# The last phase of a three-stage kernel on pairs of 512 tokens instead of 384

## The chip, the cores and the metric

The kernel runs on one core of one Trainium2 chip. The metric is the device time of one execution, in microseconds (us); the time of a version is the median of several runs. TensorE (PE) multiplies matrices, VectorE (DVE) and ScalarE (ACT) work elementwise and read TensorE's results out of PSUM, GpSimd (POOL) works elementwise on SBUF alone, and SyncE (SP) issues nearly all DMAs.

## The reference

Three stages follow each other. 4 x 768 = 3072 tokens of width 512 go through all of them.

```python
x = attention(q, k, v, mem_k, mem_v)              # chunks of 32 tokens, 16 left, 8 right, 8 memory slots
h = x @ w_in                                      # 512 -> 2048
x = (max(h, 0) + log1p(exp(-abs(h)))) @ w_out     # 2048 -> 512
out = ((x @ w_a) * (x @ w_b)) @ w_out2            # 512 -> 1536, product, 1536 -> 512
```

## The kernel before, in words

All matrix products keep float32 accuracy by splitting each operand into a high and a low part (`hi`, `lo`) and adding three products: hi x hi, hi x lo and lo x hi. So one product of a 128-row slice takes three matmuls.

The first two stages run on eight tiles of `TT` = 384 tokens. In each tile, 16 slices `f` of the hidden width are computed one after the other: `emit_h` (L538, `ph`), `emit_soft` (ACT and DVE, with the split of the result into `gh` and `gl`), and two slices later `emit_x1` (L562, `px`). Attention for the tile after is laid between them. Each tile's result goes to DRAM (`x1d`, L571).

The last phase takes the tokens in four pairs of 384 (`p` = 0..3). The product of the pair with a 2 x 2 block arrangement of `w_a` and `w_b` is done with seven block products instead of eight (a Strassen-Winograd scheme): sums of token blocks (`add_pair`, L585) and of weight blocks (`Conversion`) are formed first, and `product` (L720) does one block product as 2 x 3 = 6 matmuls. For each of the 12 slices `f` of the width 1536, `pair_step` (L767) runs, in this order on TensorE: the block products "11" (bank `x`), "s2" (`y`), "s3" (`w`), "s1" (`v`), "12" (onto `x`), "22" (onto `w`), "s4" (onto `v`). DVE combines the banks into the sums `q`, `r`, `d22`, `d21`, `d12`, forms the two products `c2` and `c1` (the gated activations of the second and the first half of the pair), and splits them, with ACT, into `c`.

The last matmul of the model is cut into jobs (`job`, L739, `py`): a job takes 128 tokens of one half and two slices `f`, and is 2 x 3 = 6 matmuls of 512 columns; DVE adds its result to `y` (L758). Every second step adds six jobs to a list, and `next_job` takes three of them per step, one each after "s2", "s1" and "22". What is left when the steps end is done in a tail. 4 pairs x 6 groups x 6 jobs make 144 jobs; the very last is cut into two of 256 columns.

In the last phase the order on every engine is the order of the code (a manual schedule). `at(k)` (L955) is called after each block product and lays other work between: for pair 0 the conversion of the weights (POOL and ACT), later the loads of the converted weights (`fetch_u`, L712) and, in the steps `f` = 6 to 11 of a pair, the loads, sums and splits of the next pair's token blocks (`load_pair`, `add_pair`, `split_hi` on ACT, `split_lo` on DVE and POOL). For pair 0 these sums and splits stand in the last tile of the second stage (`plan2`, L898), all on DVE. The last two `emit_x1` run inside step 0 of pair 0.

Of the kernel before, what the change touches and what calls it, by code (L numbers as in the profile page):

```python
# [9 lines left out]
F32 = mybir.dt.float32  # L10
# [7 lines left out]
TT = 384  # L18

# [23 lines left out]
OUT_TAGS = "eegg"  # L43
# [3 lines left out]
GROUP = 2  # L47
# [3 lines left out]
def attn_moe_moe2(ctx: ExitStack, tc: tile.TileContext, q, k, v, mem_k, mem_v,  # L51
# [17 lines left out]
    NTILE = NT // TT  # L69
    KT = DM // P  # L70
# [8 lines left out]
    x1d = nc.dram_tensor("x1_scratch", (NTILE, P, KT, TT), F32, kind="Internal").ap()  # L79
# [463 lines left out]
    def emit_soft(t, f, ph, engine=nc.gpsimd, one=None, two=None):  # L543
        e = mp.tile([P, TT], F32, tag="e", name=f"e{t}_{f}")
        nc.scalar.activation(e, ph, AF.Abs)  # L545
        nc.scalar.activation(e, e, AF.Exp, scale=-1.0)  # L546
        nc.scalar.activation(e, e, AF.Ln, bias=1.0)  # L547
        g = mp.tile([P, TT], F32, tag="g", name=f"g{t}_{f}")
        nc.vector.scalar_tensor_tensor(g, ph, 0.0, e, ALU.max, ALU.add)  # L549
        if one:  # L550
            one()
        gt[t, f] = split(g, f"g{t}_{f}", engine, two)

    def emit_x1(t, f):
        gh, gl = gt.pop((t, f))
        w = w1o[f]
        if f == 0:
            acc[t] = [ps.tile([P, 512], F32, tag=f"acc{i}", name=f"px{t}_{i}", bufs=1) for i in range(KT)]
        for i in range(KT):
            wh, wl = w[:, 0, i * P:(i + 1) * P], w[:, 1, i * P:(i + 1) * P]  # L560
            for m, (a, c) in enumerate(((wh, gh), (wh, gl), (wl, gh))):
                nc.tensor.matmul(acc[t][i][:, :TT], lhsT=a, rhs=c, start=f == 0 and m == 0,  # L562
                                 stop=f == NF1 - 1 and m == 2)
        if f == NF1 - 1:
            for i in range(KT):
                if t == NTILE - 1:
                    o = wp.tile([P, TT], F32, tag="w", name=f"xo{t}_{i}")
                else:
                    o = mp.tile([P, TT], F32, tag=OUT_TAGS[i], name=f"xo{t}_{i}")
                nc.vector.tensor_copy(o, acc[t][i][:, :TT])  # L570
                nc.sync.dma_start(x1d[t, :, i, :], o)  # L571
            del acc[t]
# [7 lines left out]
    def load_pair(p):  # L580
        for n, (t, k) in {"11": (0, 0), "12": (0, 1), "21": (1, 0), "22": (1, 1)}.items():
            raws[n] = wp.tile([P, KH, TT], F32, tag="w", name=f"x{n}_{p}")
            nc.sync.dma_start(raws[n], x1d[2 * p + t, :, KH * k:KH * k + KH, :])

    def add_pair(engine, n):  # L585
        r = raws
        if n == "s1":
            r[n] = wp.tile([P, KH, TT], F32, tag="w", name="xs1")
            engine.tensor_tensor(r[n], r["21"], r["22"], ALU.add)
        elif n == "s2":  # L590
            r[n] = wp.tile([P, KH, TT], F32, tag="w", name="xs2")
            engine.tensor_tensor(r[n], r["s1"], r["11"], ALU.subtract)
        elif n == "s3":
            r[n] = r.pop("21")
            engine.tensor_tensor(r[n], r["11"], r[n], ALU.subtract)
        else:
            r["s4"] = wp.tile([P, KH, TT], F32, tag="w", name="xs4")
            engine.tensor_tensor(r["s4"], r["12"], r["s2"], ALU.subtract)

    def split_hi(p, n, copy):  # L600
        if n in ("22", "s4"):
            if (p, "2") not in parts:
                parts[p, "2"] = mp.tile([P, 2, 2, KH, TT], F32R, tag="x", name=f"xx{p}")
            sums[p, n] = parts[p, "2"][:, n == "s4"]
        else:
            sums[p, n] = late["x"].tile([P, 2, KH, TT], F32R, tag="s", name=f"x{n}_{p}")
        copy(sums[p, n][:, 0], raws[n])
# [125 lines left out]
    def temp(tag, name):  # L733
        return mp.tile([P, TT], F32, tag=tag, name=name, bufs=3 if tag in ("gh", "gl") else 2)
# [4 lines left out]
    def job(p, m, half, i, cols=slice(0, DM)):  # L739
# [27 lines left out]
    def pair_step(p, f, at, between=()):  # L767

        late_lo = pair_step.late
        x = bank("h", f"pX{p}_{f}")  # L770
        product(x, p, f, "11", True)
        s = temp("e", f"s{p}_{f}")
        nc.scalar.copy(s, x[:, :TT])
# [3 lines left out]
        q = temp("gh", f"q{p}_{f}")  # L777
        tt(q, y[:, :TT], s, ALU.add)
# [10 lines left out]
        tt(r, w[:, :TT], q, ALU.add)  # L789
# [5 lines left out]
        d22 = temp("gl", f"d22_{p}_{f}")  # L795
        tt(d22, v[:, :TT], r, ALU.add)
# [20 lines left out]
        cs[p, f, 0] = c = wp.tile([P, 2, TT], F32R, tag="w", name=f"c{p}_{f}_0")
        nc.scalar.copy(c[:, 0], c1)  # L818
        tt(cc[:, 1], c2, cc[:, 0].bitcast(F32), ALU.subtract)
        late_lo.append(lambda: tt(c[:, 1], c1, c[:, 0].bitcast(F32), ALU.subtract))  # L820
# [6 lines left out]
    def order():  # L827
# [92 lines left out]
        for t in range(NTILE):  # L920
# [3 lines left out]
            if t == NTILE - 1:  # L924
# [4 lines left out]
                late["x"] = ctx.enter_context(tc.tile_pool(name="late", bufs=5))  # L929
# [21 lines left out]
        for p in range(NTILE // 2):  # L951
            more = p + 1 < NTILE // 2
            for f in range(NF2):

                def at(k):  # L955
# [15 lines left out]
                    if nxt[0] > 0 and nxt[0] < NTILE // 2:  # L971
# [6 lines left out]
                    if more:  # L978
# [4 lines left out]
                        if f == 9 and k in (1, 3):  # L983
                            n = "22" if k == 1 else "s4"
                            split_hi(p + 1, n, nc.scalar.copy)
                            split_lo(p + 1, n, nc.gpsimd)
                        if f == NF2 - 1:
                            if k < 5:
                                split_hi(p + 1, PRODUCTS[k], nc.scalar.copy)
                            if 0 < k < 6:  # L990
                                split_lo(p + 1, PRODUCTS[k - 1], nc.gpsimd if k in (2, 4) else nc.vector)

                pair_step(p, f, at, (between_0, between_0) if (p, f) == (0, 0) else ())
        while jobs:
            if len(jobs) == 5 and pair_step.late:
                pair_step.late.pop()()
# [38 lines left out]
```

## Time and profile before

| what | value |
| --- | --- |
| time, median of 3 runs | 1189.16 us (1187.32 to 1193.07) |
| span of the profiled execution, first to last instruction | 1185.4 us |
| PE busy (share of the span) | 1177.1 us (99%) |
| DVE, ACT, POOL busy | 734.8 (62%), 537.0 (45%), 279.5 us (24%) |
| granted TensorE clock | 1.000 of full speed, mean of the span |
| last phase, first to last matmul | 627.6 to 1181.9 us of the span |

The profiled execution has no time of its own beside its span, 1185.4 us; the median of the timed runs lies 3.8 us above it. The busy share of PE counts a matmul from its start to a modelled end, and a matmul starts before the one ahead of it has ended. So a busy share of 99% tells that PE hardly waits; how long a matmul takes is read from the distance between starts, not from the mean duration. A row of the timeline merges equal instructions that follow each other: the time at its head is the start of the first.

### The profile page before, as it was taken

How to read it: one execution, taken by the hardware profiler on the slowest of the kernel's cores; microseconds unless marked ns; L12 is line 12 of the kernel's file. 1: busy time of each engine (PE TensorE's matmuls, PEld its weight loads, DVE VectorE, ACT ScalarE, POOL GpSimd, SP SyncE). 2: the span in 40 equal slices, each digit the busy share in tenths (PEclk: the TensorE clock that was granted, in tenths of full speed). 3: DMA queues.
4: the chain of work that ended last, by engine and by line, in shares of the span. 5: the costliest groups of instructions: out<-in, count | busy, mean ns of one | idle time of the engine just before them, and what ended most of it. 6: DMA issues, size and time to landing. Idle time of an engine off the chain costs nothing.

```text
span 1185.4 us, 21520 instructions
## 1 busy us (share of the span) xinstructions
PE 1177.1 (99%) x7966; PEld 1115.2 (94%) x7966; DVE 734.8 (62%) x1707; ACT 537.0 (45%) x1329; POOL 279.5 (24%) x249
## 2 busy tenths in 40 slices
PE   9999999999999999999999999999999999999998
PEld 7899999999999999999999999999999999999997
DVE  6888654555556555465387668755666456655565
ACT  6899565655656566565564433221112211212010
POOL 2000323223232222322325778200211002100000
PEclk9999999999999999999999999999999999999999
DMA  9955334353343633432556895788554965379521
GB/s 237 295 178 111 109 86 110 93 115 107 87 107 93 120 107 84 104 97 62 178 205 238 324 341 190 267 327 298 199 196 141 375 234 183 133 255 369 194 80 54
DMA packets 198841, 209.86 MB, mean 177 GB/s; under 512 B 121632, under 2 KB 150224, under 8 KB 198736
## 3 DMA queue, kind: packets, MB, share of 16 engines
q1 hardware_dynamic: 198352, 208.43, 54.9%
q8 instruction: 63, 1.03, 0.4%
q14 instruction: 42, 0.34, 0.1%
q0 software_dynamic: 384, 0.05, 0.0%
HBM read 158.11 MB, written 50.33 MB: 176 GB/s over the span
## 4 chain that ended last, share of the span: by engine, by line
PE 93%; ACT 3%; DVE 2%; DMA 1%; issue 1%; SPq 0%; DVEq 0%; ACTq 0%
PE ph L538 21%; PE px L562 21%; PE py L749 17%; PE pW L726 8%; PE pX L726 8%; PE pV L726 8%; PE pY L726 4%; PE pxa L476 2%; PE sc L429 1%; DMA raw<-in_moe_w_in_dram 1%; DVE tmp L122 1%; ACT sm L383 1%; DMA vv<-in_v_dram 0%; ACT work L383 0%; DVE tmp L121 0%
## 5 line engine op out<-in xcount | busy, mean ns | idle before, releaser
L538 PE MATMUL ph<-x,w 128*128 128x384 f32 x1536 | 289.7, 336 | 0.1
L538 PEld LDWEIGHTS ph<-x,w 128*128 128x128 f32 x1536 | 266.7, 188 | 2.2 <-issue 0.3
L749 PE MATMUL py<-w2o,c 128*128 128x512 f32 (+1 forms) x870 | 222.2, 392 | 0.0
L549 DVE SCALAR_TENSOR_TENSOR g<-ph,e 128x384 f32<-128x384 f32 x128 | 71.3, 557 | 205.6 <-ACT e L547 205.3
L749 PEld LDWEIGHTS py<-w2o,c 128*128 128x128 f32 x870 | 160.5, 188 | 25.3
L808 ACT CAST c<-c 128x384 fp32r<-128x384 f32 x48 | 24.7, 514 | 302.4 <-DVE c L806 269.8
L726 PE MATMUL pX<-x,u 128*128 128x384 f32 x576 | 115.5, 334 | 0.0
L758 DVE TENSOR_TENSOR y<-py,y 128x512 f32<-128x512 f32 (+1 forms) x121 | 83.0, 686 | 47.3 <-PE py L749 46.9
L545 ACT ACTIVATE e<-ph 128x384 f32<-128x384 f32 x128 | 62.3, 486 | 103.9 <-PE ph L538 89.9
L726 PEld LDWEIGHTS pX<-x,u 128*128 128x128 f32 x576 | 102.1, 188 | 4.1
L447 DVE STREAM_TRANSPOSE af<-sm 32x256 f32<-32x256 f32 x180 | 78.2, 435 | 2.5
L804 DVE TENSOR_TENSOR d<-pW,q 128x384 f32<-128x384 f32 x48 | 26.7, 557 | 68.5 <-PE pW L726 68.5
L546 ACT ACTIVATE e<-e 128x384 f32<-128x384 f32 x128 | 67.3, 526 | 4.0
L547 ACT ACTIVATE e<-e 128x384 f32<-128x384 f32 x128 | 67.3, 526 | 3.8
L383 ACT ACTIVATE sm<-sm,st 128x96 f32<-128x96 f32 x168 | 60.5, 362 | 3.6 <-DVE st L379 3.6
L818 ACT CAST c<-c 128x384 fp32r<-128x384 f32 x48 | 24.6, 513 | 77.9 <-DVE c L816 76.9
L726 PE MATMUL pW<-xs,u 128*128 128x384 f32 x288 | 57.8, 335 | 0.0
L726 PE MATMUL pV<-xx,u 128*128 128x384 f32 x288 | 57.8, 335 | 0.0
L726 PE MATMUL pV<-xs,u 128*128 128x384 f32 x288 | 57.6, 334 | 0.0
L726 PE MATMUL pY<-xs,u 128*128 128x384 f32 x288 | 57.6, 334 | 0.0
L726 PE MATMUL pW<-xx,u 128*128 128x384 f32 x288 | 57.6, 334 | 0.0
L726 PEld LDWEIGHTS pV<-xx,u 128*128 128x128 f32 x288 | 51.5, 188 | 4.1
(251 smaller groups left out, 2229.3 us busy)
## 6 DMA issues: line engine op xcount, KB each, us to landing
u<-u_scratch SPq DMA_DIRECT2D x108, 512.0 KB
u_scratch<-u SPq DMA_DIRECT2D x36, 512.0 KB
w2o<-w2o_scratch SPq DMA_DIRECT2D x36, 512.0 KB
u<-u_scratch SPq DMA_DIRECT2D x36, 256.0 KB
raw<-in_moe_w_in_dram SPq DMA_DIRECT2D x16, 512.0 KB
raw<-in_moe_w_out_dram SPq DMA_DIRECT2D x16, 512.0 KB
vn<-in_v_dram SPq DMA_DIRECT2D x35, 176.0 KB
raw_a<-in_moe_w_a_dram SPq DMA_DIRECT2D x12, 512.0 KB
```

What stands on the lines that cost most here:

```text
L383: nc.scalar.activation(sm[:, h], sm[:, h], AF.Exp, bias=st[:, 0, h:h + 1], scale=-1.0, accum_out=st[:, 1, h:h + 1])
L447: nc.vector.transpose(out=af[32 * kb:32 * kb + 32, x], in_=self.sm[32 * x:32 * x + 32, :, 32 * kb:32 * kb + 32])
L538: nc.tensor.matmul(ph, lhsT=w[:, a, kt * P:(kt + 1) * P], rhs=x[:, c, kt, :], start=n == 0, stop=n == 3 * KT - 1)
L545: nc.scalar.activation(e, ph, AF.Abs)
L546: nc.scalar.activation(e, e, AF.Exp, scale=-1.0)
L547: nc.scalar.activation(e, e, AF.Ln, bias=1.0)
L549: nc.vector.scalar_tensor_tensor(g, ph, 0.0, e, ALU.max, ALU.add)
L562: nc.tensor.matmul(acc[t][i][:, :TT], lhsT=a, rhs=c, start=f == 0 and m == 0, stop=f == NF1 - 1 and m == 2)
L726: nc.tensor.matmul(bank[:, :TT], lhsT=u[:, j, a, kt * P:kt * P + P], rhs=x[:, c, kt, :], start=first_ and m == 0, stop=m == 3 * KH - 1, sk ...
L749: nc.tensor.matmul(b, lhsT=c[:, x, r], rhs=w[:, y, cols], start=n == 0, stop=n == 3 * GROUP - 1)
L758: tt(y, b, y, ALU.add)
L804: tt(d21, w[:, :TT], q, ALU.add)
```

## The change

The last phase takes pairs of `T2` = 512 tokens: three pairs instead of four, with the twelve steps each as before. Every block product has 512 columns instead of 384. A half now has four slices of 128 tokens, so a group of two steps gives eight jobs; `pair_step` takes four per step, with one more between "s3" and "s1". The jobs themselves are the same 144, of 512 columns.

To fit SBUF, the temporaries are written in place: `q` becomes `d12` and then `c1`, `r` becomes `d22` and then `c2`, and `r` and `d21` have one buffer each instead of two. The three tags `gh`, `gl`, `g` of the second stage become slices of one tile each (`turn_of`). The seven token blocks (`operand`) lie in tiles of 4 KB pieces: "11", "s2", "s3" and half of "s1" in a pool of their own, the rest in the two 12 KB buffers that held the tiles `x`, and the last half of "s4" in the place of `gh`. So "22" and "s4" are no longer split at `f` = 9 ahead of the pair's end: all seven are split in step 11, one after each block product, the low parts of "22" and "s4" on DVE. For pair 0, "22" and "s4" are split in its step 0. `x1d` in DRAM has one layout for all tokens.

```diff
+T2 = 512
@@ turn_of, split
+            rings[tag] = mp.tile([P, n, TT], dtype, tag=tag, name=tag, bufs=1)
+        return rings[tag][:, n_turn[tag] % n]
-        hi = mp.tile([P, TT], F32R, tag="gh", name=name + "h", bufs=3)
+        hi, lo = turn_of("gh", 3, F32R), turn_of("gl", 3, F32R)
@@ load_pair
-            raws[n] = wp.tile([P, KH, TT], F32, tag="w", name=f"x{n}_{p}")
-            nc.sync.dma_start(raws[n], x1d[2 * p + t, :, KH * k:KH * k + KH, :])
+            raws[n] = wp.tile([P, KH, T2], F32, tag="w", name=f"x{n}_{p}")
+            nc.sync.dma_start(raws[n], x1d[:, KH * k:KH * k + KH, c0:c0 + T2])
@@ operand (new)
+        if n in ("11", "s2", "s3"):
+            return [home(f"x{n}", late["x"], [P, KH, 2, T2], f"x{n}")]
+        if n == "s1":
+            return [home("xs1a", late["x"], [P, 1, 2, T2], "xs1"), home("xa", mp, [P, 3, 2, T2], "x")[:, 0:1]]
+        if n == "12":
+            return [home("xa", mp, [P, 3, 2, T2], "x")[:, 1:3]]
+        if n == "22":
+            return [home("xb", mp, [P, 3, 2, T2], "x")[:, 0:2]]
+        return [parts[p, "xb"][:, 2:3], home("xs4b", mp, [P, 1, 2, T2], "gh")]
@@ product
-                nc.tensor.matmul(bank[:, :TT], lhsT=u[:, j, a, kt * P:kt * P + P], rhs=x[:, c, kt, :],
+                nc.tensor.matmul(bank[:, :T2], lhsT=u[:, j, a, kt * P:kt * P + P], rhs=x[kt][:, c],
@@ pair_step
-        s = temp("e", f"s{p}_{f}")
-        nc.scalar.copy(s, x[:, :TT])
+        q = temp("e", f"q{p}_{f}")
+        nc.scalar.copy(q, x)
-        q = temp("gh", f"q{p}_{f}")
-        tt(q, y[:, :TT], s, ALU.add)
+        tt(q, y, q, ALU.add)
-        r = temp("e", f"r{p}_{f}")
+        r = temp("g", f"r{p}_{f}")
         if between:
             between[1]()
+        else:
+            next_job()
-        tt(d22, v[:, :TT], r, ALU.add)
+        tt(r, v, r, ALU.add)
-        d21 = temp("e", f"d21_{p}_{f}")
+        d21 = temp("gl", f"d21_{p}_{f}")
-        tt(c2, d21, d22, ALU.mult)
+        tt(r, d21, r, ALU.mult)
-        tt(d12, v[:, :TT], q, ALU.add)
-        tt(c1, x[:, :TT], d12, ALU.mult)
+        tt(q, v, q, ALU.add)
+        tt(q, x, q, ALU.mult)
@@ order, at(k)
-                        if f == 9 and k in (1, 3):
-                            n = "22" if k == 1 else "s4"
-                            split_hi(p + 1, n, nc.scalar.copy)
-                            split_lo(p + 1, n, nc.gpsimd)
                         if f == NF2 - 1:
-                            if k < 5:
-                                split_hi(p + 1, PRODUCTS[k], nc.scalar.copy)
-                            if 0 < k < 6:
+                            split_hi(p + 1, PRODUCTS[k], nc.scalar.copy)
+                            if k > 0:
                                 split_lo(p + 1, PRODUCTS[k - 1], nc.gpsimd if k in (2, 4) else nc.vector)
+                    if f == 0 and k == 0 and p > 0:
+                        split_lo(p, PRODUCTS[6], nc.vector)
+                    if p == f == 0 and k in (0, 2):
+                        split_hi(0, PRODUCTS[5 + k // 2], nc.scalar.copy)
+                    if p == f == 0 and k in (1, 3):
+                        split_lo(0, PRODUCTS[5 + k // 2], nc.vector)
```

On TensorE, one step of the last phase before (step 5 of the last pair; the numbers in a name are the pair's step or, in `py`, group, half and slice, and at its end a running number of the tile):

```order
L726 MATMUL pX_5_12212<-x_3_11587,u_5_0_12119 128x384 x6
L726 MATMUL pY_5_12223<-xs_3_11601,u_5_1_12131 128x384 x6
L749 MATMUL py_1_00_0_12235<-w2o_2_11867,c_2_0_12004 128x512 x3
L749 MATMUL py_1_00_0_12235<-w2o_3_11971,c_3_0_12107 128x512 x3
L726 MATMUL pW_5_12243<-xs_3_11623,u_5_2_12150 128x384 x6
L726 MATMUL pV_5_12254<-xs_3_11637,u_5_1_12131 128x384 x6
L749 MATMUL py_1_01_0_12265<-w2o_2_11867,c_2_0_12004 128x512 x3
L749 MATMUL py_1_01_0_12265<-w2o_3_11971,c_3_0_12107 128x512 x3
L726 MATMUL pX_5_12212<-x_3_11656,u_5_0_12119 128x384 x6
```

and a step of the changed kernel, from its block product "s2" on:

```order
L756 MATMUL pY_7_10863<-xs_2_9999,u_7_1_10767 128x512 x6
L779 MATMUL py_2_00_0_10874<-w2o_4_10505,c_4_0_10639 128x512 x3
L779 MATMUL py_2_00_0_10874<-w2o_5_10610,c_5_0_10744 128x512 x3
L756 MATMUL pW_7_10882<-xs_2_10021,u_7_2_10786 128x512 x6
L779 MATMUL py_2_01_0_10893<-w2o_4_10505,c_4_0_10639 128x512 x3
L779 MATMUL py_2_01_0_10893<-w2o_5_10610,c_5_0_10744 128x512 x3
L756 MATMUL pV_7_10901<-xs1a_10042,u_7_1_10767 128x512 x3
L756 MATMUL pV_7_10901<-xa_10043,u_7_1_10767 128x512 x3
L779 MATMUL py_2_02_0_10911<-w2o_4_10505,c_4_0_10639 128x512 x3
```

A job now stands between "s3" and "s1" too, and no matmul of 384 columns is left between those of 512.

On DVE, the end of pair 1 and the start of pair 2 before (`x12_2` is block "12" of pair 2; `c1_11_1` the low part of the gated activations of step 11, second half; `q2_0` the first sum of pair 2):

```order
L806 TENSOR_TENSOR c2_1_11_10399<-d21_1_11_10397,d22_1_11_10365 128x384
L611 TENSOR_TENSOR x12_2_10388<-x12_2_9861,x12_2_10388 128x768
L758 TENSOR_TENSOR y1_2_9531<-py1_4_02_0_10404,y1_2_9531 128x512
L814 TENSOR_TENSOR d12_1_11_10418<-pV1_11_10358,q1_11_10328 128x384
L816 TENSOR_TENSOR c1_1_11_10420<-pX1_11_10308,d12_1_11_10418 128x384
L819 TENSOR_TENSOR c1_11_1_10401<-c2_1_11_10399,c1_11_1_10401 128x384
L778 TENSOR_TENSOR q2_0_10443<-pY2_0_10436,s2_0_10432 128x384
```

and in the changed kernel at the same place:

```order
L836 TENSOR_TENSOR r1_11_10017<-d21_1_11_10072,r1_11_10017 128x512
L640 TENSOR_TENSOR xa_2_10043<-x12_2_9523,xa_2_10043 128x2x512
L788 TENSOR_TENSOR y1_3_9185<-py1_4_03_0_10080,y1_3_9185 128x512
L843 TENSOR_TENSOR q1_11_9982<-pV1_11_10032,q1_11_9982 128x512
L844 TENSOR_TENSOR q1_11_9982<-pX1_11_9975,q1_11_9982 128x512
L847 TENSOR_TENSOR c1_11_1_10075<-r1_11_10017,c1_11_1_10075 128x512
L640 TENSOR_TENSOR xb_2_10077<-x22_2_9527,xb_2_10077 128x2x512
L640 TENSOR_TENSOR xb_2_10077<-xs4_9733,xb_2_10077 128x512
L640 TENSOR_TENSOR xs4b_2_10099<-xs4_9733,xs4b_2_10099 128x512
L808 TENSOR_TENSOR q2_0_10110<-pY2_0_10116,q2_0_10110 128x512
```

The three splits of "22" and "s4" now stand on DVE between the last low part of pair 1 and the first sum of pair 2.

## Rows read from the trace of the kernel before

**Rows 1.** The page: busy time of the engines, and the chain that ended last.

```profile
PE 1177.1 (99%) x7966; PEld 1115.2 (94%) x7966; DVE 734.8 (62%) x1707; ACT 537.0 (45%) x1329; POOL 279.5 (24%) x249
...
PE 93%; ACT 3%; DVE 2%; DMA 1%; issue 1%; SPq 0%; DVEq 0%; ACTq 0%
```

**Rows 2.** Windows of the last phase: busy us (instructions) of PE, PEld, DVE, ACT, POOL.

```profile
627.60:749.50 121.90, 121.90 (x650) 114.74 (x650) 88.21 (x135) 45.69 (x94) 88.63 (x73) 1.00 0.76 281
749.50:887.00 137.50, 137.50 (x721) 128.00 (x721) 83.57 (x142) 26.19 (x50) 15.42 (x8) 1.00 0.72 260
...
1172.10:1181.90 9.80, 9.80 (x50) 8.16 (x48) 6.53 (x11) 0.51 (x1) 0.00 (x0) 1.00 0.29 109
```

**Rows 3.** Timeline of PE, one step: start, us from start to end, tile, count.

```profile
888.05 1.20 PE L726 MATMUL pY<-xs,u 128*128 128x384 f32 x6
889.09 1.55 PE L749 MATMUL py<-w2o,c 128*128 128x512 f32 x6
890.48 1.21 PE L726 MATMUL pW<-xs,u 128*128 128x384 f32 x6
891.52 1.20 PE L726 MATMUL pV<-xs,u 128*128 128x384 f32 x6
892.56 1.55 PE L749 MATMUL py<-w2o,c 128*128 128x512 f32 x6
893.95 1.21 PE L726 MATMUL pX<-x,u 128*128 128x384 f32 x6
...
899.51 1.20 PE L726 MATMUL pY<-xs,u 128*128 128x384 f32 x6
```

**Rows 4.** Groups by line: matmuls of block products and jobs, and the weight loads.

```profile
L726 PE MATMUL pX<-x,u 128*128 128x384 f32 x576 | 115.5, 334 | 0.0
L726 PE MATMUL pY<-xs,u 128*128 128x384 f32 x288 | 57.6, 334 | 0.0
L726 PEld LDWEIGHTS pX<-x,u 128*128 128x128 f32 x576 | 102.1, 188 | 4.1
L749 PE MATMUL py<-w2o,c 128*128 128x512 f32 x858 | 220.8, 393 | 0.0
```

**Rows 5.** Timeline of the tail: jobs on PE, the additions after them on DVE.

```profile
1172.12 9.79 PE L749 MATMUL py<-w2o,c 128*128 128x512 f32 x48
...
1177.80 0.69 DVE L758 TENSOR_TENSOR y<-py,y 128x512 f32<-128x512 f32 x1 [0.67 <-PE py L749]
1179.16 0.69 DVE L758 TENSOR_TENSOR y<-py,y 128x512 f32<-128x512 f32 x1 [0.67 <-PE py L749]
1180.52 1.14 DVE L758 TENSOR_TENSOR y<-py,y 128x512 f32<-128x512 f32 x2 [0.67 <-PE py L749]
1181.94 0.42 DVE L758 TENSOR_TENSOR y<-py,y 128x256 f32<-128x256 f32 x1 [0.29 <-PE py L749]
```

**Rows 6.** Timeline around the end of pair 1: splits, sums and low parts.

```profile
889.24 0.84 ACT L607 CAST x<-x 128x768 fp32r<-128x768 f32 x1
890.31 0.95 DVE L611 TENSOR_TENSOR x<-x,x 128x768 fp32r<-128x768 f32 x1
890.88 2.10 POOL L611 TENSOR_TENSOR xs<-xs,xs 128x768 fp32r<-128x768 f32 x1 [19.91 <-ACT xs L607]
898.17 0.68 DVE L758 TENSOR_TENSOR y<-py,y 128x512 f32<-128x512 f32 x1
898.77 0.55 DVE L814 TENSOR_TENSOR d<-pV,q 128x384 f32<-128x384 f32 x1
899.35 0.56 DVE L816 TENSOR_TENSOR c<-pX,d 128x384 f32<-128x384 f32 x1
899.83 0.55 DVE L819 TENSOR_TENSOR c<-c,c 128x384 fp32r<-128x384 f32 x1
```

**Rows 7.** Timeline of the last tile: sums of pair 0 on DVE, POOL beside them.

```profile
598.72 0.95 DVE L589 TENSOR_TENSOR xs<-x,x 128x768 f32<-128x768 f32 x1
598.80 3.99 POOL L686 TENSOR_TENSOR u<-t,u 128x512 fp32r<-128x512 f32 x2 [3.63 <-ACT u L682]
599.71 1.93 DVE L592 TENSOR_TENSOR xs<-xs,x 128x768 f32<-128x768 f32 x1
601.56 2.05 DVE L595 TENSOR_TENSOR x<-x,x 128x768 f32<-128x768 f32 x1
```

More of the change, by code (lines that the diff above doesn't have):

```diff
@@ L521, in attn_moe_moe2, with turn_of @@
     anchor = [None]
+    rings, n_turn = {}, {}
+    def turn_of(tag, n, dtype):
+        if tag not in rings:
+            rings[tag] = mp.tile([P, n, TT], dtype, tag=tag, name=tag, bufs=1)
+            n_turn[tag] = 0
+        n_turn[tag] += 1
+        return rings[tag][:, n_turn[tag] % n]
     def split(val, name, engine=nc.gpsimd, between=None):
-        hi = mp.tile([P, TT], F32R, tag="gh", name=name + "h", bufs=3)
-        lo = mp.tile([P, TT], F32R, tag="gl", name=name + "l", bufs=3)
+        hi, lo = turn_of("gh", 3, F32R), turn_of("gl", 3, F32R)
         anchor[0] = nc.scalar.copy(hi, val)
@@ L547, in emit_soft @@
         nc.scalar.activation(e, e, AF.Ln, bias=1.0)
[L548 removed]
+        g = turn_of("g", 2, F32)
         nc.vector.scalar_tensor_tensor(g, ph, 0.0, e, ALU.max, ALU.add)
@@ L568, in emit_x1 @@
                 else:
-                    o = mp.tile([P, TT], F32, tag=OUT_TAGS[i], name=f"xo{t}_{i}")
+                    o = turn_of("g", 2, F32) if i > 1 else mp.tile([P, TT], F32, tag="e", name=f"xo{t}_{i}")
                 nc.vector.tensor_copy(o, acc[t][i][:, :TT])
-                nc.sync.dma_start(x1d[t, :, i, :], o)
+                nc.sync.dma_start(x1d[:, i, TT * t:TT * t + TT], o)
             del acc[t]
@@ L596, in add_pair, with operand, home, pieces_of @@
         else:
-            r["s4"] = wp.tile([P, KH, TT], F32, tag="w", name="xs4")
+            r["s4"] = wp.tile([P, KH, T2], F32, tag="w", name="xs4")
             engine.tensor_tensor(r["s4"], r["12"], r["s2"], ALU.subtract)
-    def split_hi(p, n, copy):
[L601 to L607, printed above, removed]
+    def operand(p, n):
+        def home(key, pool, shape, tag):
+            if (p, key) not in parts:
+                parts[p, key] = pool.tile(shape, F32R, tag=tag, name=f"{key}_{p}", bufs=2 if tag == "x" else 1)
+            return parts[p, key]
+        if n in ("11", "s2", "s3"):
[7 more added lines that the diff above has]
+        return [parts[p, "xb"][:, 2:3], home("xs4b", mp, [P, 1, 2, T2], "gh")]
+    def pieces_of(p, n):
+        k = 0
+        for x in sums[p, n]:
+            yield x, raws[n][:, k:k + x.shape[1]]
+            k += x.shape[1]
+    def split_hi(p, n, copy):
+        sums[p, n] = operand(p, n)
+        for x, raw in pieces_of(p, n):
+            copy(x[:, :, 0], raw)
     def split_lo(p, n, engine):
-        x = sums[p, n]
-        engine.tensor_tensor(x[:, 1], raws[n], x[:, 0].bitcast(F32), ALU.subtract)
+        for x, raw in pieces_of(p, n):
+            engine.tensor_tensor(x[:, :, 1], raw, x[:, :, 0].bitcast(F32), ALU.subtract)
     us, w2o = {}, {}
@@ L721, in product @@
         i, j = PLACE[n]
-        u, x = us[p, f][i], sums[p, n]
+        u = us[p, f][i]
+        x = [part[:, k] for part in sums[p, n] for k in range(part.shape[1])]
         m = 0
@@ L733, in temp @@
     def temp(tag, name):
-        return mp.tile([P, TT], F32, tag=tag, name=name, bufs=3 if tag in ("gh", "gl") else 2)
+        return mp.tile([P, T2], F32, tag=tag, name=name, bufs=2 if tag == "e" else 1)
     cs, yacc, jobs, n_jobs = {}, {}, [], [0]
@@ L750, in job @@
                 n += 1
-        place = 3 * (1 - half) + i
+        place = T2 // P * (1 - half) + i
         if m == 0:
@@ L759, in job @@
             if m == NF2 // GROUP - 1:
-                r0 = (2 * p + half) * TT + i * P
+                r0 = (2 * p + half) * T2 + i * P
                 nc.sync.dma_start(out[r0:r0 + P, cols], y)
@@ L783, in pair_step @@
             between[0]()
-        elif (p, f) != (NTILE // 2 - 1, NF2 - 1):
+        elif not last:
             next_job()
@@ L802, in pair_step @@
         product(w, p, f, "22", False)
-        d21 = temp("e", f"d21_{p}_{f}")
-        tt(d21, w[:, :TT], q, ALU.add)
-        c2 = temp("gl", f"c2_{p}_{f}")
-        tt(c2, d21, d22, ALU.mult)
-        cs[p, f, 1] = cc = wp.tile([P, 2, TT], F32R, tag="w", name=f"c{p}_{f}_1")
-        nc.scalar.copy(cc[:, 0], c2)
+        d21 = temp("gl", f"d21_{p}_{f}")
+        tt(d21, w, q, ALU.add)
+        tt(r, d21, r, ALU.mult)
+        cs[p, f, 1] = cc = wp.tile([P, 2, T2], F32R, tag="w", name=f"c{p}_{f}_1")
+        nc.scalar.copy(cc[:, 0], r)
         at(5)
@@ L812, in pair_step @@
         product(v, p, f, "s4", False)
-        d12 = temp("g", f"d12_{p}_{f}")
-        tt(d12, v[:, :TT], q, ALU.add)
-        c1 = temp("g", f"c1_{p}_{f}")
-        tt(c1, x[:, :TT], d12, ALU.mult)
[L817 to L820, printed above, removed]
+        tt(q, v, q, ALU.add)
+        tt(q, x, q, ALU.mult)
+        cs[p, f, 0] = c = wp.tile([P, 2, T2], F32R, tag="w", name=f"c{p}_{f}_0")
+        nc.scalar.copy(c[:, 0], q)
+        tt(cc[:, 1], r, cc[:, 0].bitcast(F32), ALU.subtract)
+        late_lo.append(lambda: tt(c[:, 1], q, c[:, 0].bitcast(F32), ALU.subtract))
         at(6)
         if f % GROUP == GROUP - 1:
-            jobs.extend((p, f // GROUP, half, i) for half in (1, 0) for i in range(TT // P))
+            jobs.extend((p, f // GROUP, half, i) for half in (1, 0) for i in range(T2 // P))
     pair_step.late = []
@@ L907, in order @@
         pieces = [partial(add_pair, nc.vector, n) for n in ("s1", "s2", "s3", "s4")]
-        for n in PRODUCTS:
+        for n in PRODUCTS[:5]:
             pieces.append(partial(split_hi, 0, n, nc.vector.tensor_copy))
@@ L950, in order @@
             slot(k)
-        for p in range(NTILE // 2):
-            more = p + 1 < NTILE // 2
+        for p in range(NPAIR):
+            more = p + 1 < NPAIR
             for f in range(NF2):
@@ L970, in at @@
                     nxt = (p, f + 1) if f + 1 < NF2 else (p + 1, 0)
-                    if nxt[0] > 0 and nxt[0] < NTILE // 2:
+                    if nxt[0] > 0 and nxt[0] < NPAIR:
                         if k < 4:
```

19 lines of the change are left out of this document (10 added, 9 removed).

## The prediction

> **What bounds the kernel now.** I read the page first: PE is busy 99% of the span and makes up 93% of the chain that ended last, and no other engine is above 62% [rows 1]. The reader is to see that only TensorE's time counts, wherever it is fed. The windows of the last phase come second: PE is busy through every one of them, at a granted clock of 1.00, with DVE at 72% of the first pair's window and 61% of the second's [rows 2]. So the last phase is a stream of matmuls, and the question is what one costs, from start to start.
>
> The timeline of PE answers that. "s3" starts at 890.48, "s1" at 891.52, the job behind it at 892.56, the next block product at 893.95 [rows 3]. So six matmuls of 384 columns take 1.04 us, 173.3 ns each, and a job of six of 512 columns takes 1.39 us, 232 ns each. At 2.4 GHz 384 columns are 160.0 ns and 512 are 213.3 ns; the rest is 13.3 ns at 384. A step, from one "s2" to the next, is 899.51 - 888.05 = 11.46 us = 7 x 1.04 + 3 x 1.393.
>
> The tail shows what a job costs with no 384-column matmuls around it: the additions that wait for one job each start at 1177.80, 1179.16 and 1180.52, so a job takes 1.36 us, 226.7 ns for a matmul of 512 columns [rows 5]. That is 213.3 + 13.3 again. So every matmul has a fixed 13.3 ns beside its columns, and a job laid between block products of 384 costs 1.393 - 1.360 = 33 ns more than one among its like, a price of changing the width.
>
> **The change part by part.** *Block products.* Before there are 576 + 5 x 288 = 2016 matmuls of 384 columns [rows 4] (the group of 288 stands for five): 2016 x 173.3 = 349.4 us. After: 3 x 12 x 42 = 1512 of 512 columns, the same columns in all. At 226.7 ns: 342.7 us, 6.7 us less, which is 504 x 13.3 ns. This form (block product of 512) does not occur before. Its bounds: 213.3 ns, the bare columns, and 232 ns, what a matmul of a job costs in mid-run [rows 3]; that is 322.5 to 350.8 us. I take 226.7, since the rows of the tail show it for the same width in an unbroken stream, and nothing else in the step is wide enough to break it.
>
> *Jobs.* 144 before and after. 137 of them stand between block products before (45 steps x 3, and 2 in the last), the rest in the tail. Each loses its 33 ns: 4.6 us less. Step 0 of the first pair still has two `emit_x1` of 384 columns inside, so three changes of width are left, 0.1 us. The extra job between "s3" and "s1" is no extra work: four per step over 34 steps instead of three over 46. The tail has nine jobs instead of seven, which stay on PE either way.
>
> *The phase as a sum.* Before: step 0 is 66 x 0.1733 = 11.44, step 1 7.28, 45 steps of 11.46, the last 10.07, the tail 36 x 0.2267 + 12 x 0.12 = 9.6: 554.1 us, against 554.3 in the windows (627.6 to 1181.9) [rows 2]. After: 7 x 1.36 + 24 x 0.1733 = 13.68, then 9.52, 33 steps of 11 x 1.36 = 14.96, the last 13.60, the tail 8 x 1.36 + 1.44 = 12.32: 542.8 us. That is 11.3 us less, 11.2 with the three changes of width.
>
> *What has to stay hidden: DVE.* An addition of 512 columns out of PSUM takes 0.69 us, of 384 0.55, and a subtraction in SBUF 0.55 at 384 and 0.95 at 768 columns [rows 5, 6]; at 512 and 1024 this makes 0.69 and 1.22. A step then has 6 sums and 4 job additions out of PSUM and 3 operations in SBUF: 13 x 0.69 = 9.0 of 14.96 us, 60%, as before. The tightest wait of PE on it is for the low part of the second half's `c`. From the end of "s4" the chain is 0.2 + 3 x 0.69 = 2.3 us; the first job reads it in its sixth matmul, whose weight load comes 2.72 + 0.9 = 3.6 us after. In the last step no job lies ahead but the one left over, 2.3 against 2.3: I allow 0.1 us, once.
>
> *Written in place.* `r`, `d21` and `q` are written and read by DVE in its own order; the only other reader is ACT's cast, done well before the next step's `r`. On PE, "22" now comes 5.4 us after the end of "s3", whose sum DVE must have taken; before it was 3.5. I cost this at nothing; DVE's free 40% is the cover.
>
> *Pair change.* Twice, all seven splits fall into step 11 instead of five. ACT: 0.84 us at 768 makes 1.1 for each [rows 6], 7.8 us beside 1.9 us of its own: free. POOL's two low parts are 2.8 us each. DVE gets four low parts of 1.22 us and more behind them: 9.0 + 4.9 = 13.9 of 14.96 us. Counted through in DVE's order, the last low part of `c` of the pair ends 3.0 us after the end of "s4" instead of 2.3, against the 3.6 that PE allows; the splits of "22" and "s4" behind it make the first sum of the next pair some 2.7 us late, and "22" there, which needs `r`, has 2.4 us left. Value 0, bounds 0 and 1 us for each change.
>
> *Last tile and step 0.* DVE carried 4 sums and 14 splits of 768 there, now 4 and 10 of 1024: 1.04 of the columns. The last splits go into step 0, where no jobs run. There ACT's cast of the last half of "s4", in the place of `gh`, waits for the last `emit_x1`, 4.16 + 3 x 1.36 = 8.2 us into the step; ACT's casts for the conversion queue behind it, due a step later. DVE does the two low parts after `r`, by 9.6 + 0.2 + 3 x 0.69 = 11.9 us, and PE needs them from 12.4 on: no cost. Bounds 0 and 1 us, if DVE is behind. *DMA.* Weight fetches fall with the steps, from 36 to 24, and each has 14.96 us instead of 11.46. Nothing gained, since PE does not wait for them now.
>
> The sum: 1185.4 - 11.2 = 1174.2 us of span. The median of the runs lies 3.8 us over the profiled span, and I keep that: **1178 us**.
>
> **The rivals.** *1. The cost goes by columns, not by matmuls.* In mid-run 232 / 512 = 0.453 ns a column and 173.3 / 384 = 0.451 agree [rows 3]; then block products of 512 cost what jobs cost there, 1512 x 0.232 = 350.8, the jobs keep 1.393, and the time stays at 1189. Against it speak the tail's 226.7 [rows 5], and 12 matmuls of 256 columns at its end: 9.79 us less 36 x 0.2267 and 0.16 of the last one's end leave 1.47, 122 ns each, 0.48 a column, more than by columns. The tail is quiet, though (DVE at 6.5 of 9.8 us, POOL at none), so mid-run traffic could be what makes jobs dear. Chance 8%.
>
> *2. DVE becomes the bound at the pair changes.* While POOL ran two operations (598.80 to 602.79), DVE's sums took 1.93 and 2.05 us, beside 0.95 just before [rows 7]: a factor of 2.16. In step 11, low parts run on both engines. If all of DVE's operations in SBUF took this factor, its work there would be 10 x 0.69 + (3 x 0.69 + 4 x 1.22) x 2.16 = 21.9 us, 6.9 over the step, 14 us for both changes: 1189 - 11 + 14 = 1192, slower. It decides from a factor of 1.16 on, where DVE's work passes 14.96. For it: the seven splits are now in one step, and "22" and "s4" have moved from POOL to DVE. Against it: at the end of pair 1 DVE's 0.95 at 890.31 stood beside POOL's 2.10 at 890.88 and was no longer [rows 6], and POOL is busy for some 5.6 us of such a step only. Parts of it (1180 to 1184) are likelier than all of it. Chance 8%, 3% of it slower.
>
> The Trainium skill ("SBUF — State Buffer", on the shared port pair) states that a GpSimd operation and a DVE operation with two SBUF inputs exclude each other for a whole instruction; the 2.05 us of [rows 7] agree, the 0.95 of [rows 6] show that they need not meet. By that rule a low part can wait for at most one POOL operation, 2.8 us, so at most twice per change.
>
> *3. The fixed 13.3 ns is the weight load sticking out.* A load takes 188 ns [rows 4], more than the 160 of 384 columns and less than the 213.3 of 512. If it were hidden, block products would cost 1512 x 213.3 = 322.5 us, 26.9 less, and the time would be 1189.2 - 26.9 - 4.6 = 1158. Against it: the tail's matmuls of 512 columns each have a load too and take 226.7 [rows 5]. Chance 2%.
>
> The Trainium skill ("TensorE: Matmul & The Clock Gate", on the back-to-back issue gap) gives columns / 2.4 GHz + 2.5 ns for an isolated matmul. By this figure, an estimate, block products would fall only from 327.6 to 326.3 us, 1.3 us; the trace's 13.3 ns at both widths disagrees, and the measurement decides.
>
> **How the numbers follow.** The forecast has 82%; its own range is 1176 to 1180 (up to 2 us of stalls, and the runs before lie from 1.8 under to 3.9 over their median). Rival 1 has 8%, rival 2 8%, rival 3 2%. From no change it can be told from about 0.5% on, 5.9 us, that is under 1183.2 or over 1195.1. Faster: 82 + 2 of rival 3 and 3 of rival 2's lighter forms, 87%. Same: rival 1 and 2 of rival 2, 10%. Slower: 3%. The range, 1175 to 1184, takes the forecast and lighter stalls.
>
> **What would show it.** Right: block products 1.36 us from start to start, jobs 1.36 in mid-run too, steps of 14.96 us, the last phase 543 us from an unchanged start near 627.6. Wrong: block products of 1.39 (rival 1); steps 11 longer than the others, with PE idle on DVE's `c` or `r` (rival 2); 1.28 (rival 3); or a phase that starts later.

## The result and the profile after

| | before | changed |
| --- | --- | --- |
| median of the first comparison, 6 runs each | 1189.89 us (1187.32 to 1193.56) | 1176.45 us (1175.29 to 1178.86) |
| span of the profiled execution | 1185.4 us | 1174.8 us |
| last phase, first block product to the start of the last matmul | 627.6 to 1181.6 us | 628.3 to 1171.1 us |

The ratio of the times is 0.9893 [0.9872, 0.9913]: 1.1% faster. A second comparison gave 1177.91 us against 1188.14, ratio 0.9907 [0.9891, 0.9923] (below); one of its 17 runs of the kernel before took 1437.72 us at a granted clock of 0.753 and is left out of the ratio. The profiled execution of the changed kernel took 1176.61 us, 1.8 more than its span.

The page of the changed kernel answers to [rows 1]:

```profile
PE 1165.4 (99%) x7462; PEld 1048.8 (89%) x7462; DVE 725.7 (62%) x1603; ACT 532.2 (45%) x1293; POOL 264.8 (23%) x239
...
PE 95%; DMA 2%; SPq 1%; ACT 0%; DVE 0%; issue 0%
```

PE has 504 matmuls less and is still busy 99% of the span; the shares of DVE, ACT and POOL are within a point of where they were. So nothing else has become the bound. The windows of the last phase (busy us and instructions of PE, PEld, DVE, ACT, POOL, then clock, DMA share and GB/s), as in [rows 2], are now those of the first pair up to some way into its step 8, of the twelve steps from there over the first pair change (801.22), and of the next twelve, over the second:

```profile
628.28:746.67 118.39, 118.39 (x529) 98.70 (x529) 79.21 (x108) 42.76 (x82) 67.39 (x57) 1.00 0.68 247
746.67:926.20 179.53, 179.53 (x794) 148.71 (x793) 115.04 (x160) 36.50 (x61) 36.69 (x22) 1.00 0.56 201
926.20:1105.70 179.50, 179.50 (x794) 148.68 (x793) 105.07 (x154) 32.45 (x53) 5.53 (x3) 1.00 0.52 183
```

PE is busy through each window at the full granted clock; DVE is at 64% and 59% in the last two. What a step costs is read from the starts on PE, a step behind the first pair change, the counterpart of [rows 3]:

```profile
817.54 1.52 PE L756 MATMUL pY<-xs,u 128*128 128x512 f32 x6
818.90 1.52 PE L779 MATMUL py<-w2o,c 128*128 128x512 f32 x6
820.26 1.52 PE L756 MATMUL pW<-xs,u 128*128 128x512 f32 x6
821.62 1.52 PE L779 MATMUL py<-w2o,c 128*128 128x512 f32 x6
822.98 0.84 PE L756 MATMUL pV<-xs1a,u 128*128 128x512 f32 x3
823.66 0.84 PE L756 MATMUL pV<-xa,u 128*128 128x512 f32 x3
824.34 1.52 PE L779 MATMUL py<-w2o,c 128*128 128x512 f32 x6
```

Block products and jobs alike stand 1.36 us apart. From "s2" at 802.58 in the step ahead to 817.54 here are 14.96 us, and so is every step but the first two (13.79 and 9.52). From the first block product at 628.28 to the start of the last matmul at 1171.09 are 542.81 us, against 554.02 before: 11.21 us less. PE waits nowhere in the phase, the tail included, whose nine jobs are one row of 60 matmuls without a break:

```profile
1158.90 12.47 PE L779 MATMUL py<-w2o,c 128*128 128x512 f32 x60
```

What the pair change costs DVE stands on its timeline at the end of the first pair (the last two columns are the shapes and, in brackets, the idle time ahead and what ended it), beside [rows 6]:

```profile
800.03 1.22 DVE L640 TENSOR_TENSOR xa<-x,xa 128x1024 fp32r<-128x1024 f32 x1
801.17 0.68 DVE L788 TENSOR_TENSOR y<-py,y 128x512 f32<-128x512 f32 x1
801.77 0.68 DVE L843 TENSOR_TENSOR q<-pV,q 128x512 f32<-128x512 f32 x1
802.48 0.69 DVE L844 TENSOR_TENSOR q<-pX,q 128x512 f32<-128x512 f32 x1
803.09 0.68 DVE L847 TENSOR_TENSOR c<-r,c 128x512 fp32r<-128x512 f32 x1
...
806.03 0.68 DVE L808 TENSOR_TENSOR q<-pY,q 128x512 f32<-128x512 f32 x1
...
809.58 0.69 DVE L827 TENSOR_TENSOR r<-pV,r 128x512 f32<-128x512 f32 x1 [0.47 <-PE pV L756]
...
817.71 0.68 DVE L847 TENSOR_TENSOR c<-r,c 128x512 fp32r<-128x512 f32 x1
...
819.17 0.69 DVE L808 TENSOR_TENSOR q<-pY,q 128x512 f32<-128x512 f32 x1 [0.78 <-PE pY L756]
...
824.54 0.69 DVE L827 TENSOR_TENSOR r<-pV,r 128x512 f32<-128x512 f32 x1 [0.67 <-PE pV L756]
```

The reader compares each row with the one a step later, less 14.96. The low part of `c` starts at 803.09 instead of 802.75, 0.34 us late; the first sum of the next pair at 806.03 instead of 804.21, 1.8 us late, behind the three splits of "22" and "s4"; and `r` at 809.58 is on time again.

### The profile page after: what moved, and what is told of

Read it like the earlier page. It is cut to its first block, busy times and chain, and to the rows that moved or that the text cites. A ratio compares the mean times of both kernels' runs of the same rounds, so it can differ in the third digit from the quotient of the medians.

```text
span 1174.8 us, 20105 instructions
## 1 busy us (share of the span) xinstructions
PE 1165.4 (99%) x7462; PEld 1048.8 (89%) x7462; DVE 725.7 (62%) x1603; ACT 532.2 (45%) x1293; POOL 264.8 (23%) x239
## 4 chain that ended last, share of the span: by engine, by line
PE 95%; DMA 2%; SPq 1%; ACT 0%; DVE 0%; issue 0%
PE px L571 23%; PE ph L547 22%; PE py L779 17%; PE pX L756 8%; PE pW L756 8%; PE pV L756 8%; PE pY L756 4%; PE pxa L477 2%; PE sc L430 1%; DMA kp<-in_k_dram 1%; DMA raw<-in_moe_w_in_dram 1%; SPq L331 1%; SPq L328 0%; PE sc L305 0%; PE pa L466 0%; SPq L102 0%
## 5 line engine op out<-in xcount | busy, mean ns | idle before, releaser
L571 PE MATMUL px<-gh,w 128*128 128x384 f32 x1024 | 283.2, 337 | 0.0
L571 PEld LDWEIGHTS px<-gh,w 128*128 128x128 f32 x1024 | 186.7, 188 | 2.4 <-issue 0.2
L571 PE MATMUL px<-gl,w 128*128 128x384 f32 x512 | 171.2, 334 | 0.0
L538 POOL TENSOR_TENSOR gl<-g,gh 128x384 fp32r<-128x384 f32 x96 | 98.9, 1030 | 243.4 <-ACT gh L535 216.5
L535 ACT CAST gh<-g 128x384 fp32r<-128x384 f32 x128 | 65.7, 513 | 73.8 <-DVE g L558 72.6
L571 PEld LDWEIGHTS px<-gl,w 128*128 128x128 f32 x512 | 96.1, 188 | 0.1
L835 DVE TENSOR_TENSOR d<-pW,q 128x512 f32<-128x512 f32 x36 | 24.9, 691 | 69.1 <-PE pW L756 69.1
L756 PE MATMUL pX<-x,u 128*128 128x512 f32 x216 | 54.8, 389 | 0.0
L756 PE MATMUL pW<-xs,u 128*128 128x512 f32 x216 | 54.8, 389 | 0.0
L756 PE MATMUL pY<-xs,u 128*128 128x512 f32 x216 | 54.8, 389 | 0.0
```

The source lines that it names most:

```text
L756: nc.tensor.matmul(bank[:, :T2], lhsT=u[:, j, a, kt * P:kt * P + P], rhs=x[kt][:, c], start=first_ and m == 0, stop=m == 3 * KH - 1, skip_ ...
```

## The experiments

**The same kernel again, and its other edits without the width.** Two kernels were timed beside the same runs of the kernel before: the changed kernel as it is, and the changed kernel with its width put back.

```diff
-T2 = 512
+T2 = 384
-        x = bank("h", f"pX{p}_{f}")
+        x = bank("h", f"pX{p}_{f}")[:, :T2]
```

(and the same slice for the banks `y`, `w` and `v`). Expected of the repeat:

> The changed kernel again, beside the kernel before on the same chip. Theory A: the last phase is 11.2 us shorter and nothing else differs but the first loads, so a ratio of 1 - 11.2 / 1189.5 = 0.9906; steps of 14.96 us. Theory B (the first result, 13.4 us between the medians, has a second gain of some 2 us): a ratio of 0.9887, and a stretch ahead of the last phase that is shorter by 2 us in every run.

and of 384:

> The changed kernel with pairs of 384 tokens again: all of the change but the width (temporaries in place, slices of one tile, token blocks in 4 KB pieces, all seven splits in step 11, the fourth place for a job). Theory A (only the width counts): two steps of 42 x 0.1733 and six jobs of 1.393 us together, 22.92 us as before, the last phase 554 us, and the time of the kernel before within half a per cent. Theory B (a part of the gain comes from the other edits): the last phase shorter than 554 us, between 543 and 554 by the part it has.

The repeat gave the ratio 0.9907 stated above, where 0.9906 was expected; the 0.9887 of theory B lies outside its interval. Its phase is 542.81 us long again, but starts at 631.46, so nothing is gained ahead of it. With 384 the time was 1191.83 us (1188.39 to 1193.93) against 1188.14, ratio 1.0020 [1.0006, 1.0034], and the phase 555.73 us. So the in-place temporaries, the 4 KB pieces and the seven splits in one step gain nothing in the phase; its whole gain hangs on the width. They even cost a little where steps are short. PE and DVE at the first pair change of this kernel:

```profile
763.19 1.32 PE L779 MATMUL py<-w2o,c 128*128 128x512 f32 x5
765.02 0.50 PE L779 MATMUL py<-w2o,c 128*128 128x512 f32 x1 [0.51 <-DVE c L847]
```

```profile
758.66 1.43 DVE L640 TENSOR_TENSOR xs<-x,xs 128x768 fp32r<-128x768 f32 x1
760.01 1.50 DVE L728 TENSOR_TENSOR w2o<-vo,w2o 128x512 fp32r<-128x512 f32 x1
...
764.41 0.55 DVE L847 TENSOR_TENSOR c<-r,c 128x384 fp32r<-128x384 f32 x1
```

The low part of `c` ends at 764.96, and the sixth matmul of the job, which reads it, starts at 765.02: the very wait that the prediction had called the tightest. The first two DVE rows took 1.43 and 1.50 us, where the same forms take 0.95 and 0.68 elsewhere in this kernel, while POOL ran low parts (1.02 us from 758.25, 1.14 from 759.82). That step took 13.65 us instead of 12.85. In the tail the four starts after 1174.93 lie 0.45, 0.34, 0.65 and 0.34 us apart instead of 0.23, the third ahead of a matmul that waits for the low part of `c`; that is 0.86 us more. Both together make up nearly all of the 1.7 us over the 554.0 of the kernel before. At 512 the step is longer: the low part ends at 803.77 and the sixth matmul starts at 805.07, so the wait is covered.

**Block products in two halves of 256 columns.** The columns stay the same in all, the number of matmuls doubles. (The sums that this kernel leaves in the banks are not those of the reference; DVE, ACT and POOL run as many instructions as in the changed kernel, 1603, 1293 and 239.)

```diff
-                nc.tensor.matmul(bank[:, :T2], lhsT=..., rhs=x[kt][:, c],
+                for h in (slice(0, T2 // 2), slice(T2 // 2, T2)):
+                    nc.tensor.matmul(bank[:, h], lhsT=..., rhs=x[kt][:, c, h],
```

> The changed kernel with each block-product matmul of 512 columns issued as two of 256, the same columns in all. Theory A (every matmul has a fixed 13.3 ns beside its columns, and 512 columns after narrower ones pay 33 ns per job): 1512 matmuls more at 13.3 ns are 20.2 us, 135 jobs between block products pay 33 ns again, 4.5 us; steps of 84 x 0.120 + 4 x 1.393 = 15.65 us instead of 14.96, a time of 1176.5 + 24.6 = 1201 us. Theory B (the cost goes by columns, and the gain came from elsewhere): steps of 14.96 and the time of the changed kernel, 1176.5 us.

Measured: 1198.79 us (1197.64 to 1202.22), ratio to the kernel before 1.0092 [1.0063, 1.0120]; the phase took 565.53 us, 22.7 more than that of the changed kernel. On PE:

```profile
887.48 1.60 PE L757 MATMUL pY<-xs,u 128*128 128x256 f32 x12
888.91 1.55 PE L780 MATMUL py<-w2o,c 128*128 128x512 f32 x6
890.30 1.59 PE L757 MATMUL pW<-xs,u 128*128 128x256 f32 x12
891.74 1.55 PE L780 MATMUL py<-w2o,c 128*128 128x512 f32 x6
```

Twelve matmuls of 256 columns take 1.44 us, 120 ns each, and those of 512 columns 226.7: 256 columns more are 106.7 ns, 0.417 ns a column, one cycle of 2.4 GHz. What is left is the same 13.3 ns at 256, 384 and 512 columns, and 1512 more of it are 20.2 of the 22.7 us. Every matmul of these kernels has a weight load of its own, so no run tells whether the 13.3 ns belong to the matmul or to its load. A step is 15.60 us, so a job costs 1.38 here instead of the 1.393 that I had put in: the change of width costs some 20 ns after 256 columns, 33 after 384.

**The kernel before with its three jobs together.** If the 33 ns are a price of changing the width, three jobs behind each other should pay it once.

```diff
@@ pair_step of the kernel before: next_job() after "s2" and after "s1" taken out
-        if not between:
+        for _ in range(0 if between else 2 if (p, f) == (NTILE // 2 - 1, NF2 - 1) else 3):
             next_job()
```

> The kernel before (384 columns) with its three jobs of a step together behind block product 22 instead of apart. Theory A (a job is dear in mid-run because the width changes before it): one change of width per step instead of three; a run of 18 matmuls of 512 columns pays about 45 ns once instead of 33 ns three times, so a step of 7.28 + 4.08 + 0.05 = 11.41 us instead of 11.46, 2.5 us in 46 steps. Theory B (a job is dear in mid-run because of the other engines and the DMAs beside it): steps of 11.46 us.

Measured in one run: 1185.55 us; the phase took 552.63 us instead of 554.02, a step 11.427 instead of 11.460. The sign is that of the price of the width, the size half of what was expected. PE shows why:

```profile
891.10 1.20 PE L726 MATMUL pW<-xx,u 128*128 128x384 f32 x6
892.14 4.28 PE L749 MATMUL py<-w2o,c 128*128 128x512 f32 x18
896.26 1.23 PE L726 MATMUL pV<-xx,u 128*128 128x384 f32 x6
897.33 1.20 PE L726 MATMUL pX<-x,u 128*128 128x384 f32 x6
```

The 18 matmuls of the jobs take 4.12 us instead of 18 x 0.2267 = 4.08, and the block product behind them 1.07 instead of 1.04. So one long excursion to 512 columns costs 67 ns, one of six matmuls 33 [rows 3]. The price is not paid at once with the change; it is spread over the matmuls after it. Single starts in that row lie 229, 234, 235, 225, 230, 236, 229, 232 and 231 ns apart, then 227 steadily; those of the block product behind it 171, 175, 177, 185, 176 and 182, then 173.

**DVE at the pair change.** Rival 2 was about two engines that share work in step 11. Two runs changed one thing each: all low parts of step 11 on DVE, or the four jobs of each step together behind "22". The third has both edits.

```diff
@@ all on DVE: at(k), step 11
-    split_lo(p + 1, PRODUCTS[k - 1], nc.gpsimd if k in (2, 4) else nc.vector)
+    split_lo(p + 1, PRODUCTS[k - 1], nc.vector)
@@ jobs together: pair_step, next_job() after "s2", "s3" and "s1" taken out
-        if not between:
+        for _ in range(0 if between else 3 if last else 4):
             next_job()
```

> The changed kernel with the two low parts of step 11 that POOL does (s2 and s1) on DVE too. DVE then has 9.0 + 6 x 1.22 = 16.3 us of work in that step, 1.4 over its 14.96. Theory A (DVE's slack at the pair change is only some 0.6 us): the last low part of the pair's gated activations comes 4.4 to 5.4 us after the end of s4 against the 3.6 that PE allows, so PE stalls 0.8 to 1.8 us at each of the two changes, 1.6 to 3.6 us in all. Theory B (there is more slack than counted): no step longer than 14.96 us.

> The changed kernel (512 columns) with its four jobs of a step together behind block product 22. Control for the run before: with one width everywhere nothing is to be gained by laying jobs together. Theory A: steps of 14.96 us, and the time of the changed kernel within its own spread. If laying jobs together gains for another reason (fewer switches between weights and activations as stationary operand), steps shorter than 14.96.

With all low parts on DVE (1177.54 us in one run) the phase was 542.81 us, every step 14.96: no stall at all, so the expected 1.6 to 3.6 us fell. The window of step 11 of the first pair:

```profile
787.90:802.80 14.90, 14.90 (x67) 12.36 (x66) 14.04 (x21) 8.37 (x11) 0.00 (x0) 1.00 0.46 181
```

DVE is busy 14.04 of 14.90 us and PE does not notice. The same step of the changed kernel, and in it a split that stood beside GpSimd:

```profile
786.97:801.93 14.96, 14.96 (x68) 12.39 (x67) 12.57 (x18) 8.43 (x11) 5.05 (x3) 1.00 0.46 181
```

```profile
795.23 1.78 DVE L640 TENSOR_TENSOR xs<-x,xs 128x1024 fp32r<-128x1024 f32 x1
```

The 2.6 us of low parts that came over went into pieces of 0.39, 0.67 and 0.49 us in which DVE waits for PE there (ahead of 793.26, 794.62 and 798.70), and that split took 1.22 us instead of 1.78. The last low part of `c` came only 0.06 us later in the phase than in the changed kernel.

With the jobs together (1183.37 us in one run) the phase was 546.59 us. All block products and jobs have one width here, so by the width nothing should have changed. But three steps were longer, 15.57, 16.83 and 16.23 instead of 14.96, which no theory had. The longest on PE, on DVE and on POOL:

```profile
798.04 4.24 PE L779 MATMUL py<-w2o,c 128*128 128x512 f32 x18
803.86 1.66 PE L779 MATMUL py<-w2o,c 128*128 128x512 f32 x6 [1.58 <-DVE y L788]
```

```profile
796.61 2.06 DVE L640 TENSOR_TENSOR xs<-x,xs 128x1024 fp32r<-128x1024 f32 x1
798.59 1.78 DVE L728 TENSOR_TENSOR w2o<-vo,w2o 128x512 fp32r<-128x512 f32 x1
...
803.13 1.88 DVE L788 TENSOR_TENSOR y<-py,y 128x512 f32<-128x512 f32 x3
```

```profile
795.18 2.41 POOL L640 TENSOR_TENSOR xs<-xs,xs 128x1024 fp32r<-128x1024 f32 x1 [22.85 <-ACT xs L636]
797.54 2.27 POOL L640 TENSOR_TENSOR xs1a<-xs,xs1a 128x512 fp32r<-128x512 f32 x1
```

Three jobs fill their banks; the fourth waits for the first addition to `y`, which stands behind the splits on DVE. Two of these took longer than usual (2.06 us instead of 1.22, 1.78 instead of 0.69), beside GpSimd's low parts. So I took GpSimd out of step 11 in that order too:

> The changed kernel with the four jobs of a step together behind block product 22, as in the run before of that kind, and now with the two low parts of step 11 that GpSimd made (of s2, and of s1 and 12's first piece) on DVE as well. In the earlier run TensorE lost 1.87 us in step 11 of the first pair, 1.27 us in step 11 of the second, and 0.61 us in step 8 of the first, each inside the four jobs, where the fourth waits for an addition to y on DVE to free its bank. Theory A (DVE was held up by GpSimd, one instruction at a time: 2.06 us instead of 1.22, 1.78 instead of 0.69, 1.07 instead of 0.69): with GpSimd silent in step 11 DVE gives back about 2.3 us and takes up 1.22 + 2 x 0.69 = 2.6 us of low parts, most of them in time in which DVE waited for TensorE before; the d of the step starts at once behind 22 (+0.2 us), the first addition to y ends some 3.3 us after the start of the four jobs, before the fourth needs its bank at 4.08: both steps 11 fall to 14.96 us, and the stall of 0.61 us in step 8, where GpSimd makes a sum for the next pair, stays: last phase 543.4 to 543.6 us instead of 546.59. Theory B (too much work on DVE in step 11): its work there grows, so the two stalls of step 11 stay or grow by up to 2.6 us each: 546.6 to 551.8 us.

Measured in one run: 1180.93 us, phase 546.27 us, steps 15.57, 16.70 and 16.07. Theory A fell: without GpSimd the two stalls of step 11 shrank by 0.13 and 0.16 us only. DVE was no longer held there, but had 2.6 us of low parts more to do, and this run does not part the two. DVE in the first of the two steps:

```profile
790.72 0.69 DVE L808 TENSOR_TENSOR q<-pY,q 128x512 f32<-128x512 f32 x1 [0.77 <-PE pY L756]
...
800.80 1.88 DVE L788 TENSOR_TENSOR y<-py,y 128x512 f32<-128x512 f32 x3
803.25 0.69 DVE L788 TENSOR_TENSOR y<-py,y 128x512 f32<-128x512 f32 x1 [0.57 <-PE py L779]
```

From 790.72 to 800.80 DVE works without a pause on sums and splits, 10.1 us, and the additions come last. This kernel and that of the 14.04 us above do the same work on the same engines; they differ only in where the jobs stand. With the jobs between the block products there is no stall; with the jobs behind them there are 1.74 and 1.11 us of it in the two steps 11. So for the same work it is the order that makes the stall.

## Why the prediction was right, point by point

*What a matmul costs.* Right: 226.7 ns at 512 columns in mid-run too, the fixed 13.3 ns at three widths. The 6.7 us of the block products follow from that. Rival 1 (by columns) would have left the steps at 15.3 us, and falls by the 14.96 here and by the halves, which cost 22.7 us more for the same columns. Rival 3 (1.28 us a block product) falls by the 1.36.

*The jobs' 33 ns.* Right as a sum: jobs stand at 1.36 in the changed kernel, and the whole of the 4.6 us came. The reason I gave, a price per change of width, was too simple: the jobs together show that it grows with the length of the excursion, 33 ns for six matmuls and 67 for eighteen. In the prediction this touched only the three changes left in step 0, which took 13.79 us against 13.68 counted, 0.1 as allowed.

*The phase.* Counted 542.8, measured 542.81 in both profiled executions of the changed kernel; 11.2 us less, as forecast.

*DVE.* Value 0, right; no stall at either pair change, in step 0 or in the last step. The count was too dark: 0.34 us late instead of 0.7 for the low part of `c`, 1.8 instead of 2.7 for the first sum. Rival 2's mechanism is in the trace all the same. DVE and POOL of the changed kernel in step 8 of the first pair:

```profile
751.71 2.27 DVE L728 TENSOR_TENSOR w2o<-vo,w2o 128x512 fp32r<-128x512 f32 x1
753.90 0.68 DVE L835 TENSOR_TENSOR d<-pW,q 128x512 f32<-128x512 f32 x1
754.61 2.86 DVE L836 TENSOR_TENSOR r<-d,r 128x512 f32<-128x512 f32 x1
```

```profile
751.04 2.40 POOL L605 TENSOR_TENSOR x<-x,x 128x1024 f32<-128x1024 f32 x1
753.39 1.19 POOL L715 TENSOR_TENSOR u<-v,u 128x256 fp32r<-128x256 f32 x1
754.54 2.38 POOL L608 TENSOR_TENSOR xs<-x,xs 128x1024 f32<-128x1024 f32 x1
```

Both long DVE operations read SBUF alone and end some 0.54 us after the POOL operation beside them (753.98 after 753.44, 757.47 after 756.92); the 0.68 between them, which reads PSUM, is not held. That is a wait for one instruction, not a factor on all work. In these two rows it adds 3.8 us, and the step had them to spare: it took 14.96 us. In each of the two steps 11, which the rival was about, one split was held, for 0.56 us (1.78 instead of 1.22, as above). The Trainium skill ("SBUF — State Buffer", on the shared port pair) says that the loser of the pair is blocked for the whole instruction of the other and does not run slower beside it; these rows agree.

*From span to median.* This term was mis-sized. I kept 3.8 us between the median and the span; in the first comparison it was 1.65 (1176.45 - 1174.8). The span was 0.6 us over the forecast, so the median came 1.55 us under it. Where time and span of one execution are both on record, the time lies 2.1 us above the span in the kernel before (2.06 to 2.15 in 26 executions) and 1.8 in the changed one (1.74 to 1.83 in 11). So 1.7 of the 3.8 us came from a profiled execution that was short for its kernel. The 0.3 us between 2.1 and 1.8 are not the width's: with 384 columns the changed kernel has 1.8 too (1.76 to 1.85 in 12).

And "a phase that starts later" did happen, by 0.67 us in the first profile and 3.85 in the second, with nothing lost in the phase. The difference lies in the first 54 us, and a wait of PE on a transposed query tile there is a part of it. This wait in the changed kernel's first profile and in the second (us in total, times, longest):

```profile
PE ptq L294 <- DVE qn L296: 1.7, 1, 1.7
```

```profile
PE ptq L294 <- DVE qn L296: 3.1, 1, 3.1
```

In the kernel before the same place shows 0.2, and 0.9 with its jobs together. In the five experiments on the changed kernel it is 0.9 (halves), 1.1 (384), 2.4 (all low parts on DVE), 3.2 and 2.9 (jobs together, without and with that); their phases start at 627.7, 627.8, 629.2, 631.3 and 629.1. It moves from execution to execution; whether the changed kernel makes it longer on average stays open with two profiles on the other side. The two comparisons, one 2.2 us better and one 1.0 us worse than the 11.2 of the phase, give no sign of it.

*Two readings.* The windows of [rows 2] that the prediction calls the first and the second pair's end a step before those pairs do: at 749.5 the first pair's step 11 starts. DVE's 72% and 61% hold for the windows as they are, and the sum does not rest on where they end. The 0.95 of [rows 6] does not show that the two engines failed to meet: DVE's operation came first there, and POOL's, which started inside it, took 2.10 us. The same form takes 1.84 us where DVE runs nothing on SBUF alone beside it:

```profile
869.13 1.84 POOL L611 TENSOR_TENSOR xx<-xs,xx 128x768 fp32r<-128x768 f32 x1
```

So there it was GpSimd's operation that grew, by 0.26 us. The row spoke less against rival 2 than the prediction took it to.

## What to carry to other kernels

A stream of matmuls that each load their own weights has a fixed cost per instruction (13.3 ns here at 256, 384 and 512 columns); read it from the starts in a quiet stretch, and widen the instructions until a bank is full. Mixing widths costs a little for each excursion, more for a longer one (33 ns for six matmuls, 67 for eighteen), so one width throughout is worth more than the instruction count tells. Filler between block products also times the engine that empties the banks: the same work, with the filler moved to the step's end, stalled the matmuls by up to 1.9 us a step.

## What the runs showed of the hardware that was not expected

After a change of width from 384 to 512 columns the starts need nine matmuls (225 to 236 ns) until they are steady at 227. On the way back to 173 they need six (171 to 185 ns) after eighteen matmuls of 512, and two (172 and 179 ns) after six. The granted clock is 1.00 throughout. What makes them uneven no run here shows.
